# Scores of both chunks behind the carried products, in banks named one by one

## Chip, core and metric

The kernel runs on one core of a Trainium2 chip. The time is the device time of one execution in microseconds (us); that of the kernel before is the median of three runs. A profile is one further execution, recorded instruction by instruction; its own device time and the span of its instructions stand in the table below. The engines are TensorE (PE in the profile, its weight loads PEld), VectorE (DVE), ScalarE (ACT), GpSimd (POOL) and the DMA queue of SyncE (SP).

## What is computed

Two layers, one after the other, in fp32. The first is a gated linear recurrence over 768 steps in each of 4 x 8 heads of width 48; the second projects its output, runs a decaying sum over time on one half, gates with the other half and projects again.

```python
# first: q, k, v, alpha are (4, 8, 768, 48)
for t in range(S):
    state = alpha[:, :, t, :, None] * state + einsum('bhd,bhe->bhde', k[:, :, t], v[:, :, t])
    y[:, :, t] = einsum('bhd,bhde->bhe', q[:, :, t], state)
x = y.transpose(0, 2, 1, 3).reshape(B, S, H * D)           # (4, 768, 384)
# second: w_in (384, 1024), w_out (512, 384)
proj = x @ w_in
val, gate = proj[..., :512], proj[..., 512:]
for t in range(S):
    h = a * h + val[:, t]                                   # a = exp(A_log)
    ys[:, t] = h
out = (silu(gate) * ys) @ w_out
```

## The kernel before

The steps are cut into groups of 256 (two chunks of 128), three groups for each of the four batch entries, so N = 12 groups, numbered m or n. Within a group the recurrence becomes products: with P the running product of alpha, the scores of a chunk are (k / P) times (q P), masked to the lower triangle; the values are scores times v; the carried products bring in the state from before the chunk; the state is summed up from the keys, turned, times v.

The main loop (L1018) runs over n from 1 to 11. From n = 4 on a turn does this (else branch, L1083 to L1101, and L1102 to L1109):

- `scores(m, 0, 1)` for chunk 0 of the next group, m = n + 1 (L720; TensorE, 8 products, shown as 16 instructions of L727), into the PSUM banks 4 and 5, and `masks_apart` (L745): for each of two halves ScalarE copies the scores into the SBUF tile A (L749) and GpSimd multiplies A by the mask in place (L750).
- `state`, `values`, `values`, `state`, `carried`, `carried` of group n (L786, L765, L776). The values go to the double bank 2/3, the state to a bank of its own; ScalarE copies the state into S_sb (L789). In the last group of a batch entry (n = 5, 8, 11) the second state is left out, in the first (n = 6, 9) the first carried product.
- `join` (L791): ScalarE copies the result out of the bank (L795, L796) and two heads straight into xT (L800); eight transfers move the other heads to their rows of xT, four issued by SP and four by GpSimd (L807).
- `scores(m, 1, 1)` for chunk 1, again into banks 4 and 5, and its `masks_apart`; then `keys` for both chunks (L717 transposes, L718 copies; one only where m ends a batch entry).
- `ahead()`: the loads of group n + 3 and the v of n + 2 on SP. `go(4)`: four steps of `products(n + 2)` (L656), see below.
- `output(n - 1)` (L844): 8 products with w_out (L851, 16 instructions) and two copies and stores.
- four times `block(n, cc)` (L839): `project` (L814), three products for the value half and three for the gate half, each into a bank of 256 columns (L821); `hidden`, the decaying sum, a scan on VectorE that reads the value bank (L829); `gate`, a Silu on ScalarE that reads the gate bank (L836), and a product of the two in SBUF on GpSimd (L837). Behind each block one more step of `products`; behind the third, two checks of weights on VectorE (L571).

`products(n + 2)` is VectorE's work two groups ahead. Its four first steps: transpose of alpha (L660) with the small product `first` (L671); the scan of prod (L674); ratio, reciprocal and the scan of inv (L695), which read two tiles in SBUF; transpose of k (L660). The further ones multiply k by inv (L704), and transpose and multiply q.

Each engine works through its instructions in the order in which the code issues them; the order is written out by hand, and semaphores make an instruction wait for its inputs and for the release of its buffer. There are eight PSUM banks: one for the state, the pair 2/3, the pair 4/5, and 0, 1 and 6, which `mm` hands out in turn (L401, cycle 0, 1, 6) to keys, output and projections. A block takes two of the three, so each block's gate projection takes the bank of the values of the block before it: block 1's gate projection waits until block 0's value scan has read its bank.

Of the kernel before, what the change touches and what calls it, by code (L numbers as in the profile page):

```python
# [10 lines left out]
FP32 = mybir.dt.float32  # L11
U8 = mybir.dt.uint8
U32 = mybir.dt.uint32
AF = mybir.ActivationFunctionType
# [337 lines left out]
def fast(  # L352
# [21 lines left out]
    nc = tc.nc  # L374
    B, H, S, D = q.shape
    DM = H * D
    DI = moe_A_log.shape[0]
    C = 128
    G = 2
# [9 lines left out]
    def pool(name, bufs, **kw):  # L389
        return ctx.enter_context(tc.tile_pool(name=name, bufs=bufs, **kw))  # L390
# [9 lines left out]
    ps = pool("ps", 1, space=PS)  # L400
    next_mm, next_pair = itertools.cycle("016"), itertools.cycle((0, 1))  # L401

    def mm(*dims, b=None):
        b = b or next(next_mm)
        return (end_ps if b == "6" else ps).tile([C, *dims], FP32, tag=f"b{b}", name="mm")

    def pair_of(*dims, dtype=FP32, which=None):
        if next(next_pair) if which is None else which:
            return [end_ps.tile([C, *dims], dtype, tag=f"b{b}", name="pair") for b in (4, 5)]
        t = both()  # L410
        n = dims[0] * dims[1]
        return [t[:, i, 0:n].rearrange("p (x y) -> p x y", x=dims[0]).bitcast(dtype) for i in range(2)]

    def both():
        return ps.tile([C, 2, 4 * C], FP32, tag="b23", name="pair")
# [295 lines left out]
    def keys(m, c, b=None):  # L711

        if (m % NG) * G + c == NG * G - 1:
            return
        tp = mm(4, C, b=b)
        for p in range(4):
            nc.tensor.transpose(tp[:, p, :], Zs[m][:, p, 1, ds(c * C, C)], ident)  # L717
        nc.scalar.activation(ktms[c].rearrange("p a i d -> p a (i d)"), tp, AF.Copy)  # L718

    def scores(m, c, which=None):  # L720
        Z = Zs[m]
        cols = ds(c * C, C)
        sc = pair_of(4, C, which=which)
        for p in range(4):
            for i in range(2):
                rows = ds(64 * i, D)
                nc.tensor.matmul(sc[i][:, p, :], Z[rows, p, 1, cols], Z[rows, p, 0, cols], start=True, stop=True)  # L727
        As[m, c] = p3.tile([C, 2, 4, C], FP32, tag="A", name="A"), sc
# [8 lines left out]
    def mask_all():  # L737
        return mask[:, None, :].to_broadcast([C, 4, C])
# [6 lines left out]
    def masks_apart(m, c):  # L745

        A, sc = As[m, c]
        for i in range(2):
            nc.scalar.activation(A[:, i], sc[i], AF.Copy)  # L749
            nc.gpsimd.tensor_mul(A[:, i], A[:, i], mask_all())  # L750
# [37 lines left out]
        S_sbs[ch] = p2.tile([C, 4, D], FP32, tag="S_sb", name="S_sb")  # L788
        nc.scalar.activation(S_sbs[ch], st, AF.Copy)  # L789

    def join(m, engines):  # L791

        y = ys.pop(m)
        y_sb = p2.tile([C, 4, GC], FP32, tag="y_sb", name="y_sb")
        nc.scalar.activation(y_sb[:, 1::2], y[1], AF.Copy)  # L795
        nc.scalar.activation(y_sb[:, 2], y[0][:, 1], AF.Copy)  # L796
        xT = xTs[m] = p2.tile([C, NK, GC], FP32, tag="xT", name="xT")
        for h in (0, 4):
            kk, row = divmod(h * D, C)
            nc.scalar.activation(xT[ds(row, D), kk], y[0][ds(16 * h, D), 0], AF.Copy)  # L800
        for h in (1, 5, 3, 7, 2, 6):
            s, a = divmod(h, 4)
            d = 0
            while d < D:
                kk, row = divmod(h * D + d, C)
                size = min(D - d, C - row)
                engines[s].dma_start(out=xT[ds(row, size), kk], in_=y_sb[ds(64 * s + d, size), a])  # L807
                d += size


    prev_h = [None] * NI
# [27 lines left out]
    def block(n, cc):  # L839
        pv, pg = project(n, cc)  # L840
        hidden(n, cc, pv)
        gate(n, cc, pg)()

    def output(n):  # L844
        b, g = divmod(n, NG)
        if n < N - 1:
            os = [mm(DM) for c in range(G)]

        def part(ccs, c):
            for cc in ccs:  # L850
                nc.tensor.matmul(os[c], fs[n][:, cc, ds(c * C, C)], w_out[:, cc, :],  # L851
                                 start=(cc == 0), stop=(cc == NI - 1))

        def finish():
            for c in range(G):
                part(range(split, NI), c)
            for c in range(G):
                o_sb = p3.tile([C, DM], FP32, tag="o_sb", name="o_sb")
                nc.scalar.activation(o_sb, os[c], AF.Copy)  # L859
                nc.sync.dma_start(out=out[b, ds(g * GC + c * C, C), :], in_=o_sb)  # L860

        if n == N - 1:
            pieces = [(0, 0, DM), (1, 0, 2 * C), (1, 2 * C, DM - 2 * C)]
            os = [end_ps.tile([C, size], FP32, tag=f"b{b}", name="o")
                  for b, (_, _, size) in zip((4, 5, 6), pieces)]
            for i, ccs in ((0, range(NI - 1)), (1, range(1)), (0, range(NI - 1, NI)), (1, range(1, NI)),
                           (2, range(NI))):
                c, at, size = pieces[i]
                for cc in ccs:
                    nc.tensor.matmul(os[i], fs[n][:, cc, ds(c * C, C)], w_out[:, cc, ds(at, size)],  # L870
                                     start=(cc == 0), stop=(cc == NI - 1))
            return list(zip(pieces, os))
        split = NI - 1 if n else NI // 2
        for c in range(G):
            part(range(split), c)
        return finish


    SP, ACT = nc.sync, nc.scalar

    def loads(m):
        for name in "akq":
            load_raw(name, m, [SP])
# [53 lines left out]
    values(0, 0)  # L937
    state(0, 0)
    scores(0, 1)
    masks_far(0, 1)  # L940
    keys(0, 1, "1")
# [36 lines left out]
    banks = pair_of(4, C, dtype=U32)  # L978
# [39 lines left out]
    for n in range(1, N):  # L1018
        m = n + 1
        att = m < N  # L1020
        steps = products(n + 2) if n + 2 < N else iter(())

        def go(count):
            for _ in range(count):
                next(steps, None)


        def ahead():
            if n + 3 < N:
                loads(n + 3)  # L1030
            if n + 2 < N:
                load_v(n + 2, SP)

        if n < 3:
            if n == 1:
                block(n, 0)
                for times in [natural_qk(m, name, c, tp) for c in range(G)
                              for name, tp in zip("kq", pair_of(4, C))]:
                    times()
                block(n, 1)  # L1040
            ahead()
            for c in range(G):
                keys(m, c)
            for c in range(G):
                scores(m, c)
            go(1)
            for c in range(G):
                masks(m, c)
            if n == 2:
                block(n, 0)  # L1050
                go(1)
                block(n, 1)
                go(1)
            else:
                block(n, 2)
                go(1)
            state(m, 0)
            values(m, 0)
            values(m, 1)
            state(m, 1)  # L1060
            carried(m, 0)
            carried(m, 1)
            join(m, (nc.gpsimd, nc.gpsimd) if m == 2 else (SP, SP))
            if n == 2:
                go(2)
                block(n, 2)
            go(1)
            block(n, 3)
            go(10)
            output(n)()  # L1070
            continue

        if n == 3:
            for c in range(G):
                scores(m, c, 1 - c)
                masks_apart(m, c)
            for c in range(G):
                keys(m, c)  # L1080
            ahead()
            go(4)
        else:  # L1083
            if att:
                scores(m, 0, 1)
                masks_apart(m, 0)
            state(n, 0)
            values(n, 0)
            values(n, 1)
            state(n, 1)  # L1090
            carried(n, 0)
            carried(n, 1)
            join(n, (SP, nc.gpsimd))
            if att:
                scores(m, 1, 1)
                masks_apart(m, 1)
                for c in range(G):
                    keys(m, c)
            ahead()
            go(4)  # L1100
            output(n - 1)()  # L1101
        for cc in range(NI):  # L1102
            block(n, cc)
            go(1)
            if cc == 0 and n == N - 1:
                next(end, None)
            if cc == 2 and n > 3:
                for _ in itertools.islice(checks, 2):
                    pass  # L1109
        if n == N - 2:  # L1110
            end = check_end()
            next(end)
# [52 lines left out]
```

## Time and profile before

| | |
|---|---|
| median of 3 runs | 293.03 us (292.19 to 293.70) |
| profiled execution, device time | 292.72 us |
| its span | 291.0 us |
| turns n = 4 to 10, length by the chain of waits | 22.1 us each (107.32 to 262.19) |
| one product of a projection (L821), 576 instructions | 127.8 us busy |
| mask product on GpSimd (L750), shortest / median / longest | 1262 / 1274 / 3360 ns |
| transfers into xT, issue to landing, median | 1.9 us |

How to read the lines shown below: in the chain of waits a line is start, duration, engine, tile and line of code, and the number of instructions. In a timeline it is start, duration, engine, line, operation, output <- inputs with partitions x elements, and the number of instructions merged. In the windows a line is a stretch, its length, and for each engine its busy time in it (number of instructions), then TensorE's granted clock, the DMA share and GB/s. Ends of matmuls are modelled.

### The profile page before, as it was taken

The page shows a single profiled execution, that of the slowest core. Times are in us where ns is not written, and L with a number is a line of the kernel's source. Part 1 is how long each engine was busy: PE and PEld are TensorE (multiplying, and loading weights), DVE is VectorE, ACT ScalarE, POOL GpSimd, SP SyncE. Part 2 cuts the span into 40 slices and gives each one's busy share as a digit, 9 for nine tenths or more (in the row PEclk, how much of TensorE's full clock was granted, in tenths as well). Part 3 has the DMA queues.
Part 4 walks back from the last instruction along what each step waited for, and adds up shares of the span by engine and source line. Part 5 has one row for each costly group of instructions (what it writes and reads, how often), then busy time and mean ns, then how long its engine had stood idle before and what let it go on. Part 6 is the DMA issues. An engine that isn't in the chain of part 4 may idle for free.

```text
span 291.0 us, 6227 instructions
## 1 busy us (share of the span) xinstructions
PE 281.1 (97%) x2353; PEld 228.2 (78%) x2353; DVE 230.3 (79%) x263; ACT 108.5 (37%) x242; POOL 139.1 (48%) x165
## 2 busy tenths in 40 slices
PE   7699999999999999999999999999999999999994
PEld 6578877885896988788788788788788788687883
DVE  5998896999999999599999999699999990131221
ACT  2557634433341626227217216316316415213110
POOL 7147792375541869338337337527337336423020
PEclk9999999999999999999999999999999999999999
DMA  9999969999997991991991991992991500201102
GB/s 129 163 165 300 368 118 186 174 250 215 231 215 105 229 196 44 219 202 45 213 208 44 216 203 27 203 198 68 203 207 45 129 2 11 87 0 34 65 3 62
DMA packets 70734, 42.08 MB, mean 145 GB/s; under 512 B 47508, under 2 KB 69656, under 8 KB 70696
## 3 DMA queue, kind: packets, MB, share of 16 engines
q1 hardware_dynamic: 68240, 39.78, 69.3%
q0 software_dynamic: 1408, 1.62, 2.3%
q8 instruction: 20, 0.33, 0.5%
q10 hardware_dynamic: 1048, 0.20, 0.4%
q14 instruction: 18, 0.15, 0.2%
HBM read 33.33 MB, written 4.72 MB: 131 GB/s over the span
## 4 chain that ended last, share of the span: by engine, by line
PE 81%; DVE 8%; DMA 6%; issue 2%; SPq 1%; POOL 1%; ACT 0%; DVEq 0%; ACTq 0%; POOLq 0%
PE mm L821 38%; PE mm L851 18%; PE pair L727 7%; PE pair L765 6%; DMA raw_k<-in_k_dram 4%; PE st L786 3%; PE pair L776 3%; PE mm L717 3%; DMA raw_q<-in_q_dram 2%; PE o L870 2%; PE pair L605 1%; DVE Z L620 1%; DVE pair L552 1%; DVE prod L674 1%; DVE inv L691 1%
## 5 line engine op out<-in xcount | busy, mean ns | idle before, releaser
L821 PE MATMUL mm<-xT,w_in 128*128 128x256 f32 x576 | 127.8, 380 | 0.0
L821 PEld LDWEIGHTS mm<-xT,w_in 128*128 128x128 f32 x576 | 108.7, 190 | 17.5 <-issue 0.7
L837 POOL TENSOR_TENSOR f<-sg,hh 128x256 f32<-128x256 f32 x48 | 43.0, 896 | 100.0 <-ACT sg L836 79.4
L851 PE MATMUL mm<-w_out,f 128*128 128x384 f32 x176 | 59.4, 488 | 0.1
L836 ACT ACTIVATE sg<-mm 128x256 f32<-128x256 f32 x48 | 18.4, 384 | 97.9 <-PE mm L821 95.7
L829 DVE TENSOR_TENSOR_SCAN hh<-a_dec,hh,mm 128x256 f32<-128x256 f32 x32 | 23.6, 736 | 39.3 <-PE mm L821 36.0
L851 PEld LDWEIGHTS mm<-w_out,f 128*128 128x128 f32 x176 | 32.5, 190 | 21.3 <-POOL f L837 1.0
L750 POOL TENSOR_TENSOR A<-A,mask 128x512 f32<-128x512 f32 x32 | 45.2, 1436 | 8.4 <-ACT A L749 8.3
L695 DVE TENSOR_TENSOR_SCAN inv<-aT,last 128x1025 f32<-128x1025 f32 x10 | 35.7, 3568 | 0.3
L807 POOL DMA_DIRECT2D xT<-y_sb x44 | 22.6, 519 | 14.1 <-ACT y_sb L796 12.4
L674 DVE TENSOR_TENSOR_SCAN prod<-aT,first 128x1024 f32<-128x1024 f32 x10 | 27.9, 2794 | 0.3
L727 PE MATMUL pair<-Z 48*128 48x128 f32 x384 | 27.1, 283 | 0.8 <-DVE Z L704 0.3
L727 PEld LDWEIGHTS pair<-Z 48*128 48x128 f32 x384 | 23.2, 187 | 6.0 <-issue 2.4
L765 PE MATMUL pair<-A,v 128*64 128x128 f32 x352 | 21.3, 274 | 0.0
L859 ACT ACTIVATE o_sb<-mm 128x384 f32<-128x384 f32 x22 | 10.8, 491 | 28.0 <-PE mm L851 28.0
L749 ACT ACTIVATE A<-pair 128x512 f32<-128x512 f32 x32 | 17.3, 596 | 5.2 <-PE pair L727 5.1
L765 PEld LDWEIGHTS pair<-A,v 128*64 128x64 f32 x352 | 19.1, 137 | 0.0
L743 POOL TENSOR_TENSOR A<-A,mask 128x512 f32<-128x512 f32 x8 | 10.1, 1273 | 18.0 <-ACT A L742 18.0
L660 DVE STREAM_TRANSPOSE aT<-raw_a 128x1024 f32<-128x1024 f32 x9 | 18.4, 2041 | 0.0
L660 DVE STREAM_TRANSPOSE Z<-raw_k 128x1024 f32<-128x1024 f32 x9 | 18.2, 2024 | 0.0
L660 DVE STREAM_TRANSPOSE Z<-raw_q 128x1024 f32<-128x1024 f32 x9 | 18.2, 2020 | 0.0
L631 ACT ACTIVATE junk<-raw_a,minus 128x1024 bf16<-128x1024 f32 (+1 forms) x12 | 13.3, 1104 | 0.0
(125 smaller groups left out, 281.6 us busy)
## 6 DMA issues: line engine op xcount, KB each, us to landing
raw_k<-in_k_dram SPq DMA_DIRECT2D x24, 192.0 KB, 5.3
raw_q<-in_q_dram SPq DMA_DIRECT2D x24, 192.0 KB, 6.4
v<-in_v_dram SPq DMA_DIRECT2D x24, 192.0 KB, 7.1
raw_a<-in_alpha_dram SPq DMA_DIRECT2D x23, 192.0 KB, 3.9
out_dram<-o_sb SPq DMA_DIRECT2D x22, 192.0 KB, 4.0
raw_a<-in_alpha_dram SPq DMA_DIRECT2D x18, 176.0 KB, 4.3
raw_k<-in_k_dram SPq DMA_DIRECT2D x18, 176.0 KB, 5.4
raw_q<-in_q_dram SPq DMA_DIRECT2D x18, 176.0 KB, 7.0
```

What stands on the lines that cost most here:

```text
L660: nc.vector.transpose(out=to.rearrange("p h (c j) -> p h j c", j=NT), in_=raw_bufs[m % NR][name].rearrange("p h (j d) -> p h j d", d=D)[:, ...
L674: nc.vector.tensor_tensor_scan(out=prod, data0=al, data1=first.rearrange("p h n -> p (h n)"), initial=0.0, op0=ALU.mult, op1=ALU.max)
L695: nc.vector.tensor_tensor_scan(out=inv[:, ::-1], data0=aT[:, ::-1], data1=lasts[:, 0:4 * GC + 1][:, ::-1], initial=0.0, op0=ALU.mult, op1= ...
L727: nc.tensor.matmul(sc[i][:, p, :], Z[rows, p, 1, cols], Z[rows, p, 0, cols], start=True, stop=True)
L750: nc.gpsimd.tensor_mul(A[:, i], A[:, i], mask_all())
L765: nc.tensor.matmul(ys[m][i][ds(64 * s, 64), e, ds(c * C, C)], v_sb[:, c, 2 * p + i, :], A[:, i, p, :], start=(c == 0 and e == 0), stop=Fal ...
L807: engines[s].dma_start(out=xT[ds(row, size), kk], in_=y_sb[ds(64 * s + d, size), a])
L821: nc.tensor.matmul(pj, w_in[cc][vg][:, kk, :], xT[:, kk, :], start=(kk == 0), stop=(kk == NK - 1))
L829: nc.vector.tensor_tensor_scan(out=hh, data0=a_dec[:, cc:cc + 1].to_broadcast([C, GC]), data1=pv, initial=prev_h[cc][:, GC - 1:GC] if n % ...
L836: nc.scalar.activation(sg, pg, AF.Silu)
L837: return lambda: nc.gpsimd.tensor_mul(fs[n][:, cc, :], sg, hhs.pop((n, cc)))
L851: nc.tensor.matmul(os[c], fs[n][:, cc, ds(c * C, C)], w_out[:, cc, :], start=(cc == 0), stop=(cc == NI - 1))
```

## The change

In the turns from n = 4 on, the next group's scores no longer stand at the front and in the middle: state, values and carried products come first, then the first part of `join` with its transfers, then the scores of both chunks with their masks, then the keys. Chunk 0's scores go to banks 4 and 5, chunk 1's to banks 0 and 1; the keys go to banks 6 and 4, the output to 5 and 0, and the cycle for the projections starts anew in each turn with 1, 6, 0. `join` gets a second part, the two copies into xT, which is issued between the masks of the two chunks. Turn n = 11 has no next group and differs in its banks alone. The orders of the instructions on VectorE and on SP are the same as before; ScalarE's and GpSimd's follow the code.

```diff
     def mm(*dims, b=None):
         b = b or next(next_mm)
-        return (end_ps if b == "6" else ps).tile([C, *dims], FP32, tag=f"b{b}", name="mm")
+        return (end_ps if b in "456" else ps).tile([C, *dims], FP32, tag=f"b{b}", name="mm")
...
-    def scores(m, c, which=None):
+    def scores(m, c, which=None, sc=None):
         Z = Zs[m]
         cols = ds(c * C, C)
-        sc = pair_of(4, C, which=which)
+        sc = sc or pair_of(4, C, which=which)
...
-    def join(m, engines):
+    def join(m, engines, later=False):
...
-        for h in (0, 4):
-            kk, row = divmod(h * D, C)
-            nc.scalar.activation(xT[ds(row, D), kk], y[0][ds(16 * h, D), 0], AF.Copy)
+
+        def in_place():
+            for h in (0, 4):
+                kk, row = divmod(h * D, C)
+                nc.scalar.activation(xT[ds(row, D), kk], y[0][ds(16 * h, D), 0], AF.Copy)
+
+        if not later:
+            in_place()
...
+        return in_place
...
-    def output(n):
+    def output(n, banks=(None, None)):
         b, g = divmod(n, NG)
         if n < N - 1:
-            os = [mm(DM) for c in range(G)]
+            os = [mm(DM, b=b) for b in banks]
...
         else:
-            if att:
-                scores(m, 0, 1)
-                masks_apart(m, 0)
             state(n, 0)
             values(n, 0)
             values(n, 1)
             state(n, 1)
             carried(n, 0)
             carried(n, 1)
-            join(n, (SP, nc.gpsimd))
+            in_place = join(n, (SP, nc.gpsimd), later=True)
             if att:
-                scores(m, 1, 1)
+                scores(m, 0, 1)
+                masks_apart(m, 0)
+                in_place()
+                scores(m, 1, sc=[mm(4, C, b=b) for b in "01"])
                 masks_apart(m, 1)
-                for c in range(G):
-                    keys(m, c)
+                keys(m, 0, "6")
+                keys(m, 1, "4")
+            else:
+                in_place()
+            next_mm = itertools.cycle("160")
             ahead()
             go(4)
-            output(n - 1)()
+            output(n - 1, "50")()
```

## The prediction

> **What bounds the kernel now.** I read the page first (busy time, chain), then the chain of waits in order of time, then the timelines of the other engines inside one turn.
>
> ```profile
> PE 281.1 (97%) x2353; PEld 228.2 (78%) x2353; DVE 230.3 (79%) x263; ACT 108.5 (37%) x242; POOL 139.1 (48%) x165
> PE 81%; DVE 8%; DMA 6%; issue 2%; SPq 1%; POOL 1%; ACT 0%; DVEq 0%; ACTq 0%; POOLq 0%
> ```
>
> TensorE is busy for 281.1 of 291.0 us and carries 81% of the chain; what is not TensorE lies before 74 us, which the change leaves alone. One of the changed turns (n = 8) in the chain, with the scores of turn n = 3 above it:
>
> ```profile
> 93.95 1.99 PE pair L727 x32
> ```
> ```profile
> 195.82 1.09 PE pair L727 x16
> 196.91 0.60 PE st L786 x16
> 197.52 1.76 PE pair L765 x32
> 199.28 1.02 PE pair L776 x32
> 200.30 1.09 PE pair L727 x16
> 201.39 1.02 PE mm L717 x8
> 202.41 5.16 PE mm L851 x16
> 207.58 10.36 PE mm L821 x48
> ```
>
> The pieces follow without a gap, and the turn takes 22.12 us (195.82 to 217.94). So each tenth of a us between the kinds of products counts, and no other engine counts until it makes TensorE wait. How near one is to that is in the windows, the table by turn:
>
> ```profile
> 195.82:217.94 22.12, 22.12 (x187) 17.88 (x186) 21.83 (x18) 8.52 (x19) 10.60 (x12) 1.00 0.78 159
> ```
>
> Columns: turn, TensorE, weight loads, VectorE 21.83, ScalarE, GpSimd 10.60. VectorE has 0.3 us left in 22.12. Its own line in that turn:
>
> ```profile
> 198.41 0.53 DVE L671 TENSOR_TENSOR first<-aT,prod 128x4 f32<-128x4 f32 x1
> ...
> 199.10 3.19 DVE L674 TENSOR_TENSOR_SCAN prod<-aT,first 128x1024 f32<-128x1024 f32 x1
> ...
> 202.74 5.23 DVE L695 TENSOR_TENSOR_SCAN inv<-aT,last 128x1025 f32<-128x1025 f32 x1
> 207.89 2.01 DVE L660 STREAM_TRANSPOSE Z<-raw_k 128x1024 f32<-128x1024 f32 x1
> 209.75 0.67 DVE L829 TENSOR_TENSOR_SCAN hh<-a_dec,hh,mm 128x256 f32<-128x256 f32 x1
> ```
>
> against GpSimd in the same stretch, and the same two groups in turn n = 7:
>
> ```profile
> 201.25 2.04 POOL L807 DMA_DIRECT2D xT<-y_sb  x4 [1.11 <-ACT y_sb L796]
> 203.31 2.49 POOL L750 TENSOR_TENSOR A<-A,mask 128x512 f32<-128x512 f32 x2
> ```
> ```profile
> 180.46 2.29 DVE L695 TENSOR_TENSOR_SCAN inv<-aT,last 128x1025 f32<-128x1025 f32 x1
> ```
> ```profile
> 181.64 3.41 POOL L750 TENSOR_TENSOR A<-A,mask 128x512 f32<-128x512 f32 x2
> ```
>
> The scan of inv takes 2.29 us when it is first (n = 7), and then the two mask products take 3.41 instead of 2.49. In n = 8 it takes 5.23: the mask products ended at 205.80, the scan 2.16 later at 207.96. It waited for both of them. Turns 5, 6, 8, 9 are like 8 (5.23 to 5.26). The order is set by who is ready first: in n = 8 ScalarE's copy for the first mask product was done at about 202.5, before the scan's 202.74; in n = 7 at 180.83, after 180.46. VectorE is pinched by GpSimd, then, not by its own work.
>
> [...] The trace has both: the scan above waited out two, but an elementwise product came in between (it waited for the third mask product of turn 3, to 100.70, and the fourth waited for it):
>
> ```profile
> 99.53 2.25 DVE L704 TENSOR_TENSOR Z<-Z,inv 128x1024 f32<-128x1024 f32 x1
> ```
>
> [...]
>
> **The change, part by part, for turn n = 4 to 10.** T is the end of the previous turn's last projection.
>
> 1. TensorE's order. Scores of chunk 0 leave the front, both chunks' scores stand behind the carried products. Removed: two pieces of 1.09. Added: one piece of 32 instructions, 1.99 in turn 3, the same shapes. The state costs 0.60 behind scores (turn 8) and 0.60 behind a projection (the chain at 262.19), so no new price there; keys 1.02 and output 5.16 stay. Saving 2.18 - 1.99 = 0.19 a turn, 7 turns: 1.3 us. Bounds: 0.12 a turn (0.8 us) if the joint piece takes the 2.06 it took at 72.37, and 0.25 (1.8 us) if both seams vanish.
>
> 2. Banks named one by one, and the second part of join put off. Let t be the end of the carried products: T + 3.4 (5, 6, 8, 9) or T + 3.8 (4, 7, 10), from the pieces. ScalarE in order, with durations from its timeline: y_sb 0.87 to t + 0.94; A of chunk 0 (0.60 each, 1.08 for two) to t + 2.3; xT 0.76; A of chunk 1 to t + 4.1; keys 1.1. TensorE asks for bank 4 (keys of chunk 1) at t + 2.5, freed at t + 1.8; bank 5 (output) at t + 3.0, or 2.6 in turns with one key group, freed at t + 2.3; bank 0 at t + 5; banks 1 and 6 at t + 8.2, freed by t + 5.2. All covered, cost 0. The least margin is 0.3 us. If it goes, about 0.3 in three turns.
>
> 3. xT. Its transfers leave at t + 0.95 as now (SP and GpSimd queues keep their order; only mask products change sides on GpSimd) and land some 2 us after issue, near t + 5; the projection now starts at t + 8.2 instead of t + 7.3. Cost 0, with more cover. Loads on SP leave about 1.1 us earlier in a turn; nothing waits for them.
>
> 4. GpSimd's order. Now: two mask products, four transfers, two mask products. After: four transfers, then four mask products in one go. This adds a wait that the diff does not name. VectorE's order is unchanged. With no mask products in front, `first` takes 0.17 instead of 0.53 and the scan of prod 2.29 instead of 3.19: VectorE comes to the scan of inv 1.26 us earlier, T + 5.67 instead of T + 6.92. But the first copy for the mask products is now done at t + 1.8 = T + 5.2, still 0.5 ahead of the scan, and the transfers in front end at t + 3.0. So turns 5, 6, 8 and 9 meet the pattern of turn 8, with four mask products instead of two: they run from t + 3.0 by 1.24 each to t + 8.0 = T + 11.4. If the scan waits for all, it ends at T + 13.5 (before: 207.96 - 195.82 = 12.14).
>
> What is queued behind it on VectorE: the transpose of k, then the scan of block 0. That ended 2.46 us after inv (207.96 to 210.42), so T + 16.0. Who waits for it: block 1's gate projection writes the bank of block 0's values (bank 1), which that scan frees. TensorE is there at T + 11.57 + 2.59 + 1.29 = T + 15.45 (before T + 15.65, against a scan done at T + 14.6: 1.0 us of cover, all used up). Stall with 0.15 from release to matmul (72.22 to 72.37): T + 16.1 + 0.15 - 15.45 = 0.8 us. VectorE then has 10 us of queue to the turn's end and ends some 0.8 late against TensorE. In turn 7 that makes it lose the race it now wins: scan at T + 6.2, copy done at T + 5.65; four products to T + 11.8, a stall of 1.2. Turn 4 starts with VectorE 1.2 us early (no checks in turn 3): its scan starts near T + 4.5, ahead of the copies, no stall. Turn 10 has no such scan.
>
> Sum: 4 x 0.8 + 1.2 = 4.4 lost, 1.4 gained (0.19 or 0.20 by the pieces): +3.0 us on the profiled execution, 292.72 to 295.7. The median of the runs is 0.31 above that execution, so 293.03 + 3.0 = 296.0.
>
> Of the arbitration, both ends: if the scan comes in after the first mask product it ends at T + 9.8 and VectorE is 2 us better off than now, cost 0 (below 0 only if TensorE waited for VectorE now, which it doesn't); if it waits for all, 0.4 to 1.2 us in each of five turns. I take the latter, since the only scan of the trace that met two ready mask products waited for both, four times out of four, and the products that came in between were not scans.
>
> **Rivals.**
> - A, forecast: the scan waits for all four. 295.7 to 296.3 by the sum, own range 294.3 to 297.6.
> - B, faster: the scan gets in after one or two mask products, or before all. Then only step 1 counts: 293.03 - 1.4 = 291.6 (291.2 to 292.2). For it: the elementwise product at 99.53. Against: the 5.23s. It decides from the point where the scan ends before T + 12.8, since then block 0's scan is in time.
> - C: stalls in some turns only. A turn that begins late asks for the scan at T + 6.4, as the first mask product starts (t + 3.0), and could get in after it like the product at 99.53; then turns 5 and 8 stall and the others recover: -1.4 + 1.6 = +0.2, 293.2 (292.4 to 294.2).
> - D: a named bank is late (least margin 0.3): some 0.3 in three turns takes most of step 1 back, 292.5. Nothing in the timelines speaks for it.
>
> **Numbers.** Chances: A 0.55, B 0.31, C 0.10, D 0.04. A change of under 0.5% (1.5 us) is no change here, about what three runs from 292.19 to 293.7 can tell. A passes +0.5% in nearly all of its range (0.53 of 0.55) and with the top of C gives slower 0.55; B's centre is -0.48%, so a little over half of it counts as faster: 0.18; the rest is 0.27. Range: 291.5 cuts off less than half of B, 297.5 the top of A, under 2 in 10 together.
>
> **What would show it.** Right: in turns 5 to 9 a scan of inv of some 7.5 us ending with the last of four mask products plus 2.16; `first` 0.17 and prod 2.29; the scores as one piece of 1.99; gaps of 0.8 us on TensorE, put down to VectorE's scan of hh, in the middle of block 1; turns of about 22.7 instead of 22.12. Wrong: inv under 5 us and turns of 21.93 (B); gaps at keys, output or block 0 (D); or a joint scores piece over 2.18, which takes step 1 away.

## The result

| | before | after |
|---|---|---|
| median of 8 runs each | 293.09 us (292.19 to 293.70) | 291.99 us (291.29 to 292.39) |
| ratio after / before | | 0.996, 95% interval 0.9944 to 0.9975 |
| profiled execution, device time | 292.72 us | 292.39 us |
| its span | 291.0 us | 290.7 us |
| turns n = 4 to 10 in the chain of waits | 107.32 to 262.19: 154.87 us | 107.66 to 261.19: 153.53 us |

The changed kernel is faster, by 0.7 to 1.6 us, or about 0.4%. The forecast was 296.0 us, 3 us slower. What came is the rival called B: the scan of inv gets in, and only the better order on TensorE counts. The busy times and the shares of the chain, from the page of the changed kernel:

```profile
PE 279.0 (96%) x2353; PEld 226.8 (78%) x2353; DVE 211.3 (73%) x263; ACT 109.2 (38%) x242; POOL 139.2 (48%) x165
PE 81%; DVE 9%; DMA 4%; issue 2%; SPq 1%; ACT 1%; POOL 0%; DVEq 0%; ACTq 0%; POOLq 0%
```

VectorE lost 19 us of busy time (230.3 to 211.3) with the same 263 instructions. Nearly all of it stands in instructions that had waited for GpSimd, above all the scans of inv (12.7 us) and of prod (4.6 us). None of it was on the path, as the kernel with TensorE's order alone shows below. Turn n = 8 in the chain of waits:

```profile
195.40 0.60 PE st L786 x16
196.00 1.76 PE pair L765 x32
197.76 1.02 PE pair L776 x32
198.79 1.09 PE pair L727 x16
199.88 0.89 PE mm L727 x16
200.77 1.02 PE mm L717 x8
201.79 5.16 PE mm L857 x16
206.96 10.36 PE mm L827 x48
```

The second half of the scores (tile `mm`, since it now takes two of the cycle's banks) follows the first at once and takes 0.89; each half took 1.09 when it stood alone between products of other shapes. Nothing else in the list has changed its length, and there is no gap. The same turn in the windows (columns as before: turn, TensorE, weight loads, VectorE, ScalarE, GpSimd):

```profile
195.40:217.32 21.92, 21.92 (x187) 17.80 (x188) 17.90 (x18) 8.63 (x19) 11.26 (x12) 1.00 0.77 151
```

The turn is 21.92 us instead of 22.12, and VectorE is busy for 17.90 of it instead of 21.83. Where VectorE's 3.9 us went is in its timeline:

```profile
197.97 0.17 DVE L671 TENSOR_TENSOR first<-aT,prod 128x4 f32<-128x4 f32 x1
...
198.31 2.29 DVE L674 TENSOR_TENSOR_SCAN prod<-aT,first 128x1024 f32<-128x1024 f32 x1
...
201.05 2.29 DVE L695 TENSOR_TENSOR_SCAN inv<-aT,last 128x1025 f32<-128x1025 f32 x1
203.26 2.06 DVE L660 STREAM_TRANSPOSE Z<-raw_k 128x1024 f32<-128x1024 f32 x1
208.36 0.75 DVE L835 TENSOR_TENSOR_SCAN hh<-a_dec,hh,mm 128x256 f32<-128x256 f32 x1 [3.05 <-PE mm L827]
```

and in GpSimd's:

```profile
199.74 2.05 POOL L812 DMA_DIRECT2D xT<-y_sb  x4 [2.88 <-ACT y_sb L796]
201.81 6.29 POOL L750 TENSOR_TENSOR A<-A,mask 128x512 f32<-128x512 f32 x4
```

The scan of inv takes 2.29 us instead of 5.23. The four mask products take 6.29 together where 4.95 would do, as in turn n = 10, which has no such scan: the first of them waited for the scan (2.60 instead of 1.28 in the trace). So in this turn the wait changed sides, and on GpSimd's side nobody is late. VectorE's scan of block 0 now waits 3.05 us for TensorE, where the forecast had TensorE wait for that scan.

What the forecast rested on can be seen failing in turn n = 5 of the changed kernel. ScalarE, VectorE and GpSimd there, one timeline after the other:

```profile
134.11 1.09 ACT L749 ACTIVATE A<-pair 128x512 f32<-128x512 f32 x2 [0.18 <-PE pair L727]
```
```profile
135.25 2.29 DVE L695 TENSOR_TENSOR_SCAN inv<-aT,last 128x1025 f32<-128x1025 f32 x1
```
```profile
136.01 6.29 POOL L750 TENSOR_TENSOR A<-A,mask 128x512 f32<-128x512 f32 x4
```

The first of the two copies, the input of the first mask product, ended at 134.71, half a us ahead of the scan's start at 135.25. The scan went first all the same. In the kernel before, in each of the four turns with a long scan, the copy was done only 0.20 to 0.23 us ahead of the scan's start, and there the scan lost, that is, it waited for the mask products. The four transfers stand in front of the mask products on GpSimd in both cases, so the next questions were how close the scan had come to losing, and what decides.

### The profile page after: what moved, and what is told of

Same layout as the page of the kernel before. It is cut to its first block, busy times and chain, and to the rows that moved or that the text cites. A ratio compares the mean times of both kernels' runs of the same rounds, so it can differ in the third digit from the quotient of the medians.

```text
span 290.7 us, 6236 instructions
## 1 busy us (share of the span) xinstructions
PE 279.0 (96%) x2353; PEld 226.8 (78%) x2353; DVE 211.3 (73%) x263; ACT 109.2 (38%) x242; POOL 139.2 (48%) x165
## 4 chain that ended last, share of the span: by engine, by line
PE 81%; DVE 9%; DMA 4%; issue 2%; SPq 1%; ACT 1%; POOL 0%; DVEq 0%; ACTq 0%; POOLq 0%
PE mm L827 38%; PE mm L857 18%; PE pair L765 6%; PE pair L727 5%; PE st L786 3%; PE pair L776 3%; PE mm L717 3%; PE mm L727 2%; DMA raw_q<-in_q_dram 2%; PE o L876 2%; DMA raw_k<-in_k_dram 2%; DVE prod L674 2%; SPq L445 1%; PE pair L605 1%; DVE pair L552 1%
## 5 line engine op out<-in xcount | busy, mean ns | idle before, releaser
L843 POOL TENSOR_TENSOR f<-sg,hh 128x256 f32<-128x256 f32 x48 | 40.4, 843 | 87.7 <-ACT sg L842 62.8
L750 POOL TENSOR_TENSOR A<-A,mask 128x512 f32<-128x512 f32 x32 | 47.7, 1521 | 5.5 <-ACT A L749 5.4
L674 DVE TENSOR_TENSOR_SCAN prod<-aT,first 128x1024 f32<-128x1024 f32 x10 | 23.4, 2338 | 0.3
L695 DVE TENSOR_TENSOR_SCAN inv<-aT,last 128x1025 f32<-128x1025 f32 x10 | 22.9, 2294 | 0.3
L727 PE MATMUL pair<-Z 48*128 48x128 f32 x272 | 18.9, 282 | 0.5 <-DVE Z L704 0.3
L727 PEld LDWEIGHTS pair<-Z 48*128 48x128 f32 x272 | 16.3, 187 | 3.3 <-issue 2.2
L743 POOL TENSOR_TENSOR A<-A,mask 128x512 f32<-128x512 f32 x8 | 10.1, 1273 | 17.7 <-ACT A L742 17.7
L835 DVE TENSOR_TENSOR_SCAN hh<-a_dec,mm 128x256 f32<-128x256 f32 x16 | 10.8, 675 | 8.6 <-PE mm L827 7.0
L786 PEld LDWEIGHTS st<-v,ktm 128*64 128x64 f32 x320 | 11.4, 137 | 3.5 <-issue 3.5
```

What stands on the lines that cost most here:

```text
L674: nc.vector.tensor_tensor_scan(out=prod, data0=al, data1=first.rearrange("p h n -> p (h n)"), initial=0.0, op0=ALU.mult, op1=ALU.max)
L695: nc.vector.tensor_tensor_scan(out=inv[:, ::-1], data0=aT[:, ::-1], data1=lasts[:, 0:4 * GC + 1][:, ::-1], initial=0.0, op0=ALU.mult, op1= ...
L786: nc.tensor.matmul(st[ds(64 * i, 64), p, :], ktms[c][:, p, i, :], vs[m % NV][:, c, 2 * p + i, 0:D], start=(ch == 0 and p == 0), stop=(ch = ...
L835: nc.vector.tensor_tensor_scan(out=hh, data0=a_dec[:, cc:cc + 1].to_broadcast([C, GC]), data1=pv, initial=prev_h[cc][:, GC - 1:GC] if n % ...
L843: return lambda: nc.gpsimd.tensor_mul(fs[n][:, cc, :], sg, hhs.pop((n, cc)))
```

## The experiments

**A later scan.** A small memset on VectorE, of a tile that nothing reads, stands ahead of the scan of inv, 1, 2, 4 or 8 times. TensorE and GpSimd keep the order of the changed kernel.

```diff
         nc.vector.reciprocal(inv_end, end)
+        for _ in range(K if m >= 6 else 0):
+            nc.vector.memset(idle, 0.0)           # idle: 128 x 192, float32
```

K = 1:

> The changed kernel with one small memset (about 0.25 us) on VectorE between the reciprocal and the scan of inv, in the products of groups 6 to 11; the results do not change. The scan then starts some 0.05 us after the last of GpSimd's four transfers has started (turns 5, 6, 8, 9), instead of 0.24 before it. Theory 'place in GpSimd's queue' (a scan that comes when only the last transfer stands in front loses to the mask products behind it and waits for all of them): scans of about 7.6 us in turns 5, 6, 8, 9, gaps of 0.8 us on TensorE in block 1, and 295 to 296.5 us in all. Theory 'fair' (the scan waits at most for the product under way): scans of at most 4.3 us, no gap, 292.0 us. Theory 'too early anyway' (0.25 us is no difference): scans of 2.29.

K = 2:

> As the run with one memset, with two (about 0.5 us): the scan starts some 0.3 us after the last transfer's start and 0.2 us ahead of the first mask product. 'Place in the queue': scans of about 7.4 us in turns 5, 6, 8, 9, perhaps 7 too, 295 to 296.5 us. 'Fair': at most 4.1 us, 292.0 us.

K = 4:

> As the run with one memset, with four (about 0.9 us): the scan starts some 0.15 us after the first mask product has started, with three more behind it. 'Place in the queue': 7 us, 295 to 296.5 us, as in the two others. 'Fair': it gets in after the first product, like the elementwise product in turn 3, about 3.5 us, 292.0 us. If the runs with one and two memsets show long scans and this one a short one, it is the transfers in front that make the scan lose, not the mask products as such.

Measured, each against the kernel before on the same chip in the same runs (median 293.3 us of 36): K = 1 291.74 us, ratio 0.9943 (0.9929 to 0.9956); K = 2 295.31 us, ratio 1.0073 (1.005 to 1.0096); K = 4 296.33 us, ratio 1.0105 (1.007 to 1.014). The first memset adds little: with K = 1 the scan comes only 0.09 us later (201.14 instead of 201.05), so that run put the scan where it still wins and says nothing of a longer delay. With K = 2 it comes 0.41 us later in the turn than in the changed kernel (6.06 us behind the turn's start instead of 5.65), and the forecast's picture appears. VectorE, GpSimd and TensorE in turn n = 8 of the kernel with two memsets:

```profile
203.53 7.45 DVE L698 TENSOR_TENSOR_SCAN inv<-aT,last 128x1025 f32<-128x1025 f32 x1
```
```profile
201.81 2.05 POOL L815 DMA_DIRECT2D xT<-y_sb  x4 [2.88 <-ACT y_sb L799]
203.88 4.95 POOL L753 TENSOR_TENSOR A<-A,mask 128x512 f32<-128x512 f32 x4
```
```profile
213.49 2.86 PE L830 MATMUL mm<-xT,w_in 128*128 128x256 f32 x12 [0.57 <-DVE hh L838]
```

The scan takes 7.45 us, ends 2.15 us after the last mask product (203.88 + 4.95 = 208.83, 203.53 + 7.45 = 210.98), and TensorE waits 0.57 us in the middle of the blocks for the scan of hh. The starts of turns 5, 7, 8 and 10 in the chain of waits of the same kernel:

```profile
130.03 0.60 PE st L789 x16
...
175.52 0.60 PE st L789 x16
...
197.47 0.60 PE st L789 x16
...
242.95 0.60 PE st L789 x16
```

Turns 5 and 6 take 45.49 us together, 8 and 9 take 45.48; in the changed kernel both pairs take 43.86 and 43.85. Turn 7, where the scan got in (2.23 us at 181.76), takes 21.95. That is 0.81 us for each lost turn, four times, 3.26 in all, and the medians agree: 295.31 - 291.99 = 3.3, from two sets of runs. In turn 8 the gap that the trace shows is 0.57 of the 0.81; the rest stands in it as longer matmuls, whose ends are modelled.

So the margin by which the scan wins is small. The starts of the scan and of GpSimd's fourth transfer, from the traces, ordered by how far ahead the scan is:

| kernel, turn | scan starts | fourth transfer starts | scan ahead | scan takes |
|---|---|---|---|---|
| before, n = 7 | 180.46 | 181.12 | 0.66 | 2.29 |
| after, n = 5 | 135.25 | 135.49 | 0.24 | 2.29 |
| after, n = 8 | 201.05 | 201.29 | 0.24 | 2.29 |
| one memset, n = 8 | 201.14 | 201.29 | 0.15 | 2.23 |
| two memsets, n = 7 | 181.76 | 181.86 | 0.10 | 2.23 |
| before, n = 6 | 158.47 | 158.55 | 0.08 | 5.26 |
| before, n = 8 | 202.74 | 202.79 | 0.06 | 5.23 |
| two memsets, n = 8 | 203.53 | 203.36 | -0.17 | 7.45 |

By these starts the edge lies between 0.10 and 0.08 us ahead of the fourth transfer's start, in all turns of these four kernels that came near it. A scan behind a memset takes 2.23 instead of 2.29, so its recorded start may stand some 0.06 us later than the others', and the edge is known no better than that. The mask product follows the fourth transfer's start by 0.5 us, so the same edge is about 0.6 us ahead of its recorded start; in these turns the two readings can't be told apart. The order of copy and scan does not separate the rows: the copy was done first in turn 8 of the changed kernel, which won, and of the kernel before, which lost.

**A scan that comes in the middle of the run.** With K = 4 the scan starts when the first mask product is already under way:

```profile
205.52 6.35 DVE L698 TENSOR_TENSOR_SCAN inv<-aT,last 128x1025 f32<-128x1025 f32 x1
```
```profile
204.77 4.94 POOL L753 TENSOR_TENSOR A<-A,mask 128x512 f32<-128x512 f32 x4
```

It does not get in after that one: it ends at 211.87, 2.16 after the fourth product. Here turn 7 loses its scan as well, as the forecast had it: the seven turns take 158.07 us, 4.54 more than in the changed kernel (forecast 4.4), and turn 7 takes 1.27 more than there (forecast 1.2). With K = 8:

> The changed kernel with eight memsets (about 2.4 us) on VectorE ahead of the scan of inv in the products of groups 6 to 11; results unchanged. The scan starts near T + 8.0, inside the second of four mask products, behind transfers. 'Transfers in front make the run one piece': it waits to T + 11.4 and takes about 5.5 us; gaps on TensorE, 295 to 298 us. 'Late in the run it gets in': 3 us, 292 to 293.5.

Measured 296.39 us, ratio 1.0111 (1.0081 to 1.0142), against 293.26 us of the kernel before. In turn 8 the scan starts at 207.66, inside the second product (that one from 206.85), and again waits to the end of the run:

```profile
207.66 5.07 DVE L698 TENSOR_TENSOR_SCAN inv<-aT,last 128x1025 f32<-128x1025 f32 x1
```
```profile
205.61 4.95 POOL L753 TENSOR_TENSOR A<-A,mask 128x512 f32<-128x512 f32 x4
```

So here four products that stand back to back behave as one piece.

**What lets an instruction in between?** In turn 3 of the kernel before, an elementwise product had come in between two mask products (2.25 us at 99.53; the median of its kind is 1.20). Either a scan is treated otherwise, or something about these mask products differs. What differs is the four transfers ahead of them. First all eight transfers of `join` go to SP, in the changed kernel and in the kernel before:

```diff
-            in_place = join(n, (SP, nc.gpsimd), later=True)
+            in_place = join(n, (SP, SP), later=True)
```

> The changed kernel with all eight transfers into xT issued by SP, none by GpSimd (turns 4 to 11). The mask products then start as soon as their copies are done, about T + 5.15, ahead of the scan of inv at T + 5.65, and stand back to back to about T + 10.1. 'Fair': the scan waits for the first product alone, 2.9 us. 'A scan waits out every mask product': 6.6 us, ending at T + 12.2, still in time for block 1. Time: 292.0 +- 0.5 in both if the last transfer, issued at t + 5.6 and landing at t + 7.5, stays hidden behind the projection's start at t + 8.2; if not, up to 0.5 us a turn more.

Measured 292.74 us, ratio 0.999 (0.9978 to 1.0002). VectorE and GpSimd in turn 8:

```profile
199.94 1.25 DVE L681 TENSOR_TENSOR ratio<-prod,last 128x4 f32<-128x4 f32 x1
201.22 0.18 DVE L687 RECIPROCAL last<-prod 128x4 f32<-128x4 f32 x1
201.44 3.10 DVE L695 TENSOR_TENSOR_SCAN inv<-aT,last 128x1025 f32<-128x1025 f32 x1
```
```profile
199.90 6.95 POOL L750 TENSOR_TENSOR A<-A,mask 128x512 f32<-128x512 f32 x4 [3.72 <-ACT A L749]
```

Now the mask products come first, 1.9 us earlier. The scan meets the second one, and gets in behind it: it ends at 204.54 while the run goes on to 206.85. The third product takes the wait (3.26 us). The small product `ratio` got in behind the first one in the same way, 1.25 instead of 0.17. The same in the kernel before:

> The kernel before with all eight transfers into xT issued by SP in turns 4 to 11, none by GpSimd. 'Seam': VectorE may get far ahead and the time stays 293.2 +- 0.4, since TensorE's order is unchanged. 'VectorE relieved': scans of inv under 3.5 us instead of 5.23 and about 292. [...] with no transfer in front, 'transfers in front make the run of mask products one piece' has the scan get in after the first mask product of chunk 1 (about 3.3 us); 'who is ready first' has it wait for both (about 4.5 us).

Measured 294.22 us, ratio 1.0032 (1.0017 to 1.0048):

```profile
202.57 3.34 DVE L695 TENSOR_TENSOR_SCAN inv<-aT,last 128x1025 f32<-128x1025 f32 x1
```
```profile
202.49 4.49 POOL L750 TENSOR_TENSOR A<-A,mask 128x512 f32<-128x512 f32 x2 [2.52 <-ACT A L749]
```

The scan waits for the one product under way and not for both (3.34 instead of 5.23). So a scan can come in between. Both kernels got slower by it, by 0.8 and 1.0 us of the medians, and this has nothing to do with the scan: turns 4 to 10 take 153.53 and 154.87 us, as without the edit. The last turn is longer, where SP has all eight transfers to issue and the projection waits for xT. In the changed kernel:

```profile
269.66 3.28 PE L827 MATMUL mm<-xT,w_in 128*128 128x256 f32 x12 [0.41 <-DMA xT<-y_sb]
```

From the last turn's start to the end of TensorE's last product are 25.63 us instead of 24.56 here, and 25.63 instead of 24.54 in the kernel before.

Then GpSimd keeps its four transfers, but comes to rest before the mask products: they are issued behind all four copies and begin with the one whose copy is last, with the eight memsets so that the scan meets them. The question is whether the scan gets in after the first product or waits for all four.

```diff
-                masks_apart(m, 0)
+                copies(m, 0)
                 in_place()
                 scores(m, 1, sc=[mm(4, C, b=b) for b in "01"])
-                masks_apart(m, 1)
+                copies(m, 1)
+                for c, i in ((1, 1), (1, 0), (0, 0), (0, 1)):
+                    A = As[m, c][0]
+                    nc.gpsimd.tensor_mul(A[:, i], A[:, i], mask_all())
```

> As the run with eight memsets, but all four mask products are issued behind ScalarE's four copies and in the order that starts with the copy that is done last (T + 7.35), one us after the transfers have ended (T + 6.4). So the same transfers stand in front of the same four products, but GpSimd has come to rest in between. Theory [...]: the scan at T + 8.0 gets in after the first product, about T + 8.7, and takes about 2.9 us; 292 to 293 us. Theory [...]: to T + 12.4, about 6.5 us, 296 us and more.

Measured 291.40 us, ratio 0.9933 (0.9912 to 0.9954). VectorE and GpSimd in turn 8:

```profile
204.00 2.88 DVE L698 TENSOR_TENSOR_SCAN inv<-aT,last 128x1025 f32<-128x1025 f32 x1
```
```profile
200.31 2.05 POOL L820 DMA_DIRECT2D xT<-y_sb  x4 [2.86 <-ACT y_sb L804]
203.47 6.95 POOL L1113 TENSOR_TENSOR A<-A,mask 128x512 f32<-128x512 f32 x4 [1.11 <-ACT A L758]
```

As with K = 4, the scan starts inside the first of four products. Between transfers and products GpSimd now rests 1.11 us, and the scan gets in after that first product: 2.88 us where the other took 6.35. (The order of the four products differs too; nothing speaks for its mattering.) In these runs, then, neither the scan nor the number of products makes the run one piece, but transfers directly in front of it.

Turn 7 of the same kernel also says something of the edge:

```profile
181.80 2.23 DVE L698 TENSOR_TENSOR_SCAN inv<-aT,last 128x1025 f32<-128x1025 f32 x1
```
```profile
181.97 6.81 POOL L1113 TENSOR_TENSOR A<-A,mask 128x512 f32<-128x512 f32 x4 [1.11 <-ACT A L758]
```

Here the scan is only 0.18 us ahead of the first product's recorded start, and goes first. That product's input, ScalarE's last copy, was done at 181.82, so it can't have begun more than 0.15 us before its recorded start. So the 0.6 us found above isn't a fixed distance from a mask product's recorded start; it belongs to products that stand directly behind transfers.

**TensorE's order alone.** The scores of chunk 0 and their copies go back to the front of the turn; the banks, the second part of `join` and GpSimd's order stay (its two products of chunk 0 still stand behind the transfers). `copies` is the ScalarE half of `masks_apart`.

```diff
             if att:
+                scores(m, 0, 1)
+                copies(m, 0)
             state(n, 0)
...
             in_place = join(n, (SP, nc.gpsimd), later=True)
             if att:
-                scores(m, 0, 1)
-                masks_apart(m, 0)
+                for i in range(2):
+                    A = As[m, 0][0]
+                    nc.gpsimd.tensor_mul(A[:, i], A[:, i], mask_all())
                 in_place()
```

> TensorE's order of the kernel before (chunk 0's scores at the turn's front), the rest of the change kept: GpSimd's transfers ahead of all four mask products, named banks, the second part of join put off. Theory 'seam' (the gain is the one change of shape saved on TensorE, 0.19 us a turn): scores are two pieces of 1.09 again, turns of 22.1, and the time is that of the kernel before, 293.2 +- 0.4. Theory 'VectorE relieved' (the gain comes from VectorE's scans no longer waiting for GpSimd): scans of 2.29 as in the changed kernel and 292.0.

Measured 292.97 us, ratio 0.9997 (0.9983 to 1.0012). Turn 8 in the windows, and its two pieces of scores in the chain:

```profile
195.90:218.01 22.11, 22.11 (x186) 17.88 (x186) 17.92 (x18) 8.51 (x19) 10.19 (x12) 1.00 0.77 153
```
```profile
195.90 1.09 PE pair L727 x16
...
200.37 1.09 PE mm L727 x16
```

VectorE is relieved as in the changed kernel (17.92 us, all scans of inv 2.29), and the turn is still 22.11. So the 3.9 us that VectorE gained are worth nothing, and the whole gain comes from the scores standing together: one seam, that is, one change between kinds of products, is saved.

**The banks alone.** Chunk 1's scores go back to banks 4 and 5, behind chunk 0's.

```diff
-                scores(m, 1, sc=[mm(4, C, b=b) for b in "01"])
+                scores(m, 1, 1)
```

> The changed kernel with chunk 1's scores in banks 4 and 5 again, as chunk 0's; nothing else changed. TensorE comes to them at t + 1.1, but ScalarE's copies free bank 4 at t + 1.8 and bank 5 at t + 2.3. If the named banks are what makes the joint piece possible: a gap of about 1.2 us behind chunk 0's scores in each of turns 4 to 10, 8 us in all, near 300 us. If TensorE has the slack: 292.

Measured 305.62 us, ratio 1.0442 (1.042 to 1.0464). Turn 8 in the chain of waits, from the scores on:

```profile
205.75 1.14 PE pair L727 x16
206.89 0.59 ACT A L749
207.48 0.04 issue
207.52 0.48 PE pair L727 x2
208.01 0.00 issue
208.01 1.16 PE pair L727 x14
209.17 1.14 PE mm L717 x8
```

TensorE waits for ScalarE's copies in the middle of the joint piece: from their start to the start of the keys are 3.42 us here against 1.98 in the changed kernel. So without other banks for the second half the new order loses more than it can gain. The expectation was too low, some 300 us. The seven turns take 13.2 us more than in the changed kernel, and the scores account for some 7 x 1.44 = 10.1 of it, if every turn is like turn 8. The rest comes behind them, since keys and output still use banks 4 and 5: keys and output get a little longer, and in turns 4, 7 and 10 the output waits for ScalarE's copies too (gaps of 0.47 us).

**Late mask products without a pause.** The order of the eight-memset kernel above, without memsets:

> The changed kernel with the four mask products behind ScalarE's four copies, the last copy's product first (the order of the run d8_late), without a pause. GpSimd rests between its transfers and the products, so the scan of inv cannot meet them behind transfers. Expected: scans of 2.29, no gaps, the same time as the changed kernel, 292.0 +- 0.4, since TensorE waits for neither; only the distance to the slow outcome grows, which the time does not show.

Measured 291.34 us, ratio 0.9943 (0.9923 to 0.9963), the scans 2.29. The interval overlaps with the changed kernel's, so it is not shown to be faster, and its turns 4 to 10 take 153.53 us as there; no version here beats the changed kernel by more than can be measured. But it does not hang on a margin: with eight memsets ahead of the scan, 2.49 us of them in the trace, TensorE still had no gap.

## Why the prediction was wrong

Step 1, TensorE's order, was right in place and size. Forecast: 2.18 down to 1.99, 0.19 a turn, 1.3 us. Measured: 1.09 + 0.89 = 1.98, and 154.87 - 153.53 = 1.34 us over seven turns in the chain of waits. The kernel with only this step undone is back at the time of the kernel before. Why a seam costs this was tested by no run.

Steps 2 and 3, banks and xT, were right at cost 0: after 100 us the trace of the changed kernel has no gap on TensorE. What the named banks are there for was shown from the other side, by 305.62 us with both halves of the scores in banks 4 and 5.

Step 4, GpSimd's order, failed. Its times were right: in turn 8, T is 195.40, the copy was done at T + 5.10 (forecast 5.2), the scan came at T + 5.65 (forecast 5.67), the transfers ended at T + 6.4 (forecast t + 3.0, with t = T + 3.4). Its mechanism and its price were right too, once the scan does lose: two memsets made the forecast's scan of some 7.5 us and the forecast's 0.8 us a turn (0.81), and with four of them the whole time is 296.33 us, where the forecast said 296.0. What failed is the sentence that says who loses, "the order is set by who is ready first", with the copy as the sign of being ready. In four turns of the changed kernel the copy was 0.44 to 0.55 us ahead and the scan went first, in 2.29 us. In the kernel before, two things happened within 0.3 us in each lost turn: the copy ended (202.51 in turn 8) and GpSimd began its last transfer (202.79), with the scan in between (202.74). I took the copy for the cause; the runs with memsets and with other queues in front point to the transfers. The working even had the numbers: the transfers end at T + 6.4 and the scan comes at T + 5.67, so the product whose input was ready still stood in GpSimd's queue behind the transfers. The input was the wrong sign to look at.

The place in the queue alone would have put the edge at the end of the transfers. The edge found is some 0.6 us ahead of the product's recorded start, about when the fourth transfer begins, so a lost scan has the earlier recorded start of the two. What happens inside GpSimd there no trace shows, and the cause of this edge stays open.

Where the scan and the mask products met, either side could be the one that waited: the scan took 2.29 beside a first product of 2.60 in turn 8 of the changed kernel, and 7.45 beside products that kept their length (4.95 for four) with two memsets. Nor did a wait behind transfers end with one product: the 5.23 us cover two of them, the 7.45 four. And by the recorded starts, to start first does not mean to win behind transfers: in turn 8 of the kernel before the scan's 202.74 is ahead of the product's 203.31, and it lost.

The rival B was given 0.31, with the elementwise product of turn 3 for it and the four lost scans against. Both were true readings; they differ in the transfers in front, whose part in this the forecast did not weigh. Rivals C and D left no trace.

## What to carry to other kernels

Before saying which of two engines' instructions waits for the other, look at what stands in front of each in its own queue, and not only at when its input is ready. Even the time at which it reaches the head of the queue was not enough here: the edge was some 0.6 us ahead of it. And when the trace shows wins and losses, list all events near the edge, since two that fall together can't be told apart by it. A gain on an engine that the chain of waits doesn't show can be worth nothing: here VectorE was freed of 3.9 us in turn 8, which without TensorE's new order left the time as it was (ratio 0.9997), and the kernel's gain came from 0.2 us a turn at TensorE's seams. Where a result rests on a margin of some tenths of a us, make the margin visible by moving one side: the changed kernel's scan is 0.24 us ahead where it needs about 0.1, and when it came 0.41 us later the time was 3.3 us longer.

## What was not expected of the hardware

- With mask products directly behind GpSimd's transfers, a scan that started 0.08 us or less before the last transfer's start waited for every mask product (5.26 us with two, in turn 6 of the kernel before; 7.45 with four, in turn 8 with two memsets); one that started 0.10 us before it waited for none (2.23, turn 7 with two memsets).
- Mask products directly behind GpSimd's transfers held VectorE out for their whole run, even when the scan came within the second of four (5.07 us in turn 8 with eight memsets). With no transfers in front, or after a rest of 1.11 us, the scan got in after the product under way (2.88 to 3.34 us in turn 8 of three kernels), or first when it started 0.18 us ahead of the first product (2.23).
- Sixteen score instructions took 1.09 us behind another shape and 0.89 behind their own (turn 8 of the two kernels).
